# Another execution list for a fused gated-recurrence and GEGLU kernel: which engine runs a step, and in which order all steps are issued

## The chip, the cores and the metric

One Trainium2 chip, one core. The metric is device time of one execution in microseconds, lower is better. The kernel's five queues are TensorE (PE), VectorE (DVE), ScalarE (ACT), GpSimd (POOL) and SyncE (SP); SP and POOL issue the transfers, which 16 DMA engines carry out.

## The reference

Two stages. The first is a recurrence over time with a complex decay, for 4 batches x 8 heads, 768 steps, head size 48:

```python
mag = np.sqrt(a_re * a_re + a_im * a_im)
scale = np.minimum(mag, 0.999) / (mag + 1e-06)
a_re_n, a_im_n = (a_re * scale, a_im * scale)
...
for t in range(S):
    new_re = ar * S_re - ai * S_im
    new_im = ar * S_im + ai * S_re
    S_re, S_im = (new_re + kv, new_im)          # kv = outer(k_t, v_t)
    y[:, :, t] = np.einsum('bhd,bhde->bhe', q[:, :, t], S_re)
```

Its output, as 3072 rows of 384, is x of the second stage (weights 384 x 1536 twice, 1536 x 384, 384 x 384):

```python
gelu = 0.5 * g * (1.0 + erf(g * inv_sqrt2))     # g = x @ w_gate
ffn_out = gelu * (x @ w_val) @ w_out
res_gate = 1.0 / (1.0 + np.exp(-(x @ w_res)))
return (x + res_gate * ffn_out).astype(np.float32)
```

## The kernel before

Time is cut into 6 chunks of 128 rows. A (batch, chunk) pair is a tile of 128 rows by 384 columns, and the 24 tiles are grouped into 14 **units**: units 0 and 1 are chunk 0 of batches 0 and 1, one tile each; unit 2 is chunk 0 of batches 2 and 3; units 3 to 11 have two tiles each, chunk by chunk, batches 0 and 1 and then 2 and 3; units 12 and 13 are the last chunk of batches 2 and 3, one tile each. Every unit goes through three functions, which record steps and don't run them:

- `prepare(p)`: SP loads ar, ai, q, k and v (one transfer of 192 KB for each tile; a letter a or b after the unit names the tile). ACT and DVE make the logarithm of the magnitude and the angle (steps ln, exp, tai, sq, lnb, la, lh, ll, atan, th, tl). PE sums both over the chunk by a triangular matrix (cumL for the logarithm, cumT for the angle; each takes a high and a low part, lh and ll, th and tl). ACT takes exponentials of the sums (pexpE, pexpI), a rounded angle (round, then fr on DVE) and sine and cosine (sin). DVE scales q and k (qe) and spreads them over cosine and sine (feat). For units below 8, PE transposes these features (peT, copied by cpT); from unit 8 on SP does it by transposing transfers (dT). mrd and mrc fetch a chunk's last decay row, carry adds the last angle of the chunk before into the next (both are transfers issued by POOL), vcast converts v.
- `attend(p)`: scores (qk), masking (am), the output of the chunk (av) and its copy (x), the state for the next chunk (kv, U, M, Mc, Gb, Gf).
- `forward(p)`: the transpose of x (peX and cpX for units 0 to 2, SP's dX after that), 12 gv steps of a unit (6 pairs, for w_gate and w_val, L606), gelu (L611) and h (L612), the residual gate (res, tanh), the output product (out, L632), ot (L636), otx (L639) and the store.

`weights()` comes first: POOL issues wg and wv in halves of three pieces of 192 KB each (steps 0 to 11; here wg01 is piece 1 of half 0 of w_gate), wr (step 12) and three pieces of wo (13 to 15). A gv step needs all three pieces of its half.

So there are 1450 steps, numbered as recorded. The order in which they are issued is written out by hand in `ORDER`, and `PLACE` says for steps that could run on several engines which one does. `Plan.run` walks `ORDER`: it gives each tile the buffer of its tag that came free first (25 wide buffers of 128 x 768 for the inputs and intermediates, 8 banks of PSUM), loads ACT's table set where a step needs another one than is loaded ("L" logarithm and exponential, "T" sine and arctangent, "G" gelu and tanh), and issues the step. An engine runs its steps in list order, and a step waits for what it reads and for the readers of the buffer that it takes. Beside that there are turns at a port: steps of the kinds in `PORT` on DVE and POOL wait for the other engine's last such step in the list:

```python
if t.kind in PORT and t.eng in ("DVE", "POOL"):
    other = turn.get("POOL" if t.eng == "DVE" else "DVE")
    if other is not None:
        after(ins, other)
    turn[t.eng] = ins
```

POOL's queue in the first 70 us, by the list (th of unit 5 is th5; tl4 is its low part for unit 4):

```
th0 tl1 mrd1 mrd0 carry3 carry3 wg12 wg11 tl3 carry4 vcast1 tai5 tl4 wg10 wg01 wg02 mrd2 wr mrd3
carry5 wg00 wv00 vcast3 th5 wv10 wv01 tl5 mrc3 wv11 wv12 wv02 wo13 tai6 mrd4 wo14 Gf3 wo15 tai7 ...
```

Of the kernel before, what the change touches and what calls it, by code (L numbers as in the profile page):

```python
# [30 lines left out]
    33: "ACT", 35: "POOL", 50: "DVE", 51: "DVE", 64: "ACT", 114: "DVE", 117: "POOL", 121: "DVE", 129: "ACT", 131: "DVE",  # L31
    134: "ACT", 140: "DVE", 145: "ACT", 190: "DVE", 191: "DVE", 203: "ACT", 213: "DVE", 221: "ACT", 223: "DVE", 227: "DVE",
    228: "DVE", 236: "DVE", 245: "DVE", 305: "DVE", 306: "DVE", 322: "ACT", 323: "POOL", 330: "DVE", 338: "ACT", 340: "DVE",
    422: "DVE", 423: "DVE", 435: "ACT", 438: "ACT", 439: "POOL", 456: "DVE", 460: "DVE", 463: "ACT", 469: "DVE", 479: "DVE",
    554: "POOL", 555: "POOL", 562: "DVE", 572: "DVE", 576: "DVE", 667: "ACT", 670: "POOL", 671: "POOL", 678: "DVE", 686: "ACT",
    692: "DVE", 695: "ACT", 711: "DVE", 783: "ACT", 786: "POOL", 787: "POOL", 794: "DVE", 802: "ACT", 804: "DVE", 821: "DVE",
    872: "DVE", 899: "DVE", 902: "POOL", 903: "POOL", 933: "DVE", 943: "DVE", 978: "DVE", 984: "DVE", 1011: "ACT", 1014: "POOL",
    1033: "DVE", 1035: "ACT", 1050: "DVE", 1088: "DVE", 1124: "POOL", 1125: "POOL", 1132: "DVE", 1143: "ACT", 1198: "DVE",
    1232: "POOL", 1251: "ACT", 1257: "DVE", 1263: "DVE", 1298: "DVE", 1324: "POOL", 1329: "DVE", 1338: "DVE", 1376: "DVE",
    1396: "POOL", 1397: "POOL", 1448: "DVE",  # L40
}
ORDER = [
    97, 98, 16, 17, 102, 103, 294, 180, 179, 104, 105, 21, 178, 293, 22, 106, 23, 107, 24, 25, 295, 296, 108, 26, 109, 110, 34,
    115, 116, 27, 35, 36, 28, 111, 303, 411, 410, 181, 29, 117, 188, 304, 118, 37, 31, 305, 412, 413, 306, 30, 119, 189, 113,
    120, 190, 307, 420, 112, 421, 308, 191, 38, 422, 32, 99, 100, 526, 528, 19, 18, 319, 39, 527, 20, 309, 40, 320, 204, 423,
    114, 122, 321, 125, 310, 8, 436, 41, 42, 205, 7, 314, 182, 529, 300, 121, 124, 123, 44, 206, 192, 126, 207, 43, 46, 322,
    193, 128, 424, 208, 129, 49, 194, 210, 642, 101, 643, 183, 184, 298, 297, 185, 302, 311, 45, 127, 50, 130, 195, 199, 196,
    47, 315, 33, 536, 211, 425, 313, 212, 209, 131, 323, 52, 135, 48, 51, 437, 213, 316, 312, 201, 200, 198, 197, 537, 132, 133,
    324, 137, 56, 136, 57, 538, 141, 54, 138, 214, 134, 53, 55, 139, 327, 325, 216, 58, 438, 299, 645, 301, 326, 140, 142, 439,
    59, 328, 215, 144, 63, 539, 143, 329, 330, 218, 64, 6, 1, 552, 331, 145, 332, 333, 217, 220, 2, 644, 187, 186, 219, 60, 443,  # L50
    440, 334, 540, 335, 652, 441, 226, 222, 341, 336, 221, 202, 12, 317, 553, 0, 3, 345, 653, 62, 442, 223, 342, 227, 61, 759,
    758, 337, 338, 444, 343, 554, 224, 339, 233, 344, 225, 231, 77, 69, 81, 9, 4, 242, 232, 555, 318, 166, 445, 340, 85, 240,
    760, 79, 71, 234, 150, 168, 73, 83, 241, 10, 152, 75, 158, 146, 11, 5, 203, 446, 426, 228, 243, 350, 170, 65, 154, 148, 87,
    67, 13, 156, 364, 761, 171, 559, 235, 427, 541, 160, 89, 560, 162, 654, 90, 431, 351, 236, 164, 348, 428, 561, 349, 244,
    354, 358, 70, 355, 245, 365, 429, 155, 430, 346, 352, 432, 157, 359, 360, 655, 434, 433, 14, 414, 159, 66, 361, 347, 353,
    74, 78, 229, 656, 72, 68, 357, 415, 230, 237, 76, 768, 15, 417, 239, 151, 249, 86, 769, 80, 82, 246, 362, 88, 161, 770, 147,
    153, 250, 149, 238, 84, 251, 556, 668, 91, 163, 252, 771, 669, 416, 167, 557, 363, 657, 165, 448, 784, 447, 558, 367, 261,
    253, 247, 563, 265, 277, 92, 785, 562, 542, 658, 248, 169, 366, 875, 874, 172, 564, 877, 876, 93, 449, 173, 273, 94, 450,
    174, 255, 275, 278, 451, 419, 262, 274, 263, 452, 457, 369, 458, 267, 670, 254, 459, 453, 786, 671, 531, 175, 460, 276, 368,
    884, 435, 455, 266, 476, 474, 885, 264, 454, 987, 418, 530, 532, 477, 475, 456, 772, 886, 268, 257, 269, 279, 270, 466, 271,  # L60
    259, 280, 1097, 986, 1096, 543, 773, 390, 370, 382, 887, 646, 533, 1207, 461, 384, 675, 374, 256, 467, 1099, 386, 774, 392,
    272, 372, 676, 95, 480, 258, 464, 672, 376, 677, 544, 547, 388, 775, 659, 260, 787, 546, 545, 481, 465, 387, 371, 660, 673,
    548, 549, 663, 674, 375, 478, 565, 662, 661, 1206, 96, 468, 287, 1106, 664, 678, 479, 1098, 989, 566, 469, 665, 281, 1107,
    567, 282, 288, 283, 573, 484, 568, 647, 389, 900, 679, 680, 176, 485, 571, 462, 569, 373, 377, 572, 1108, 391, 289, 534,
    394, 988, 284, 570, 648, 290, 996, 681, 383, 463, 649, 666, 901, 1216, 378, 396, 393, 483, 997, 575, 291, 385, 580, 486,
    502, 1217, 535, 574, 576, 998, 498, 581, 380, 504, 397, 582, 590, 177, 1213, 1306, 583, 902, 591, 788, 779, 683, 500, 488,
    789, 592, 470, 506, 487, 356, 395, 999, 791, 593, 490, 792, 285, 577, 471, 790, 379, 776, 689, 508, 492, 903, 489, 381, 793,
    690, 594, 404, 888, 595, 1311, 650, 292, 764, 1208, 651, 765, 550, 682, 685, 584, 405, 881, 684, 781, 586, 406, 601, 889,
    585, 777, 691, 780, 778, 686, 482, 687, 503, 600, 692, 551, 578, 398, 499, 907, 794, 890, 472, 762, 1105, 763, 587, 579,
    1000, 891, 708, 399, 407, 286, 589, 706, 400, 796, 688, 795, 501, 709, 878, 588, 494, 904, 491, 610, 908, 707, 1012, 408,  # L70
    693, 473, 401, 909, 493, 505, 1209, 1378, 510, 628, 606, 1013, 612, 782, 798, 511, 496, 512, 696, 614, 602, 698, 1001, 797,
    513, 629, 883, 905, 618, 697, 402, 604, 667, 622, 906, 620, 699, 1218, 712, 608, 1109, 495, 995, 880, 879, 766, 1307, 409,
    713, 616, 611, 497, 1379, 1214, 767, 596, 624, 892, 895, 710, 694, 507, 619, 613, 1014, 597, 1015, 700, 894, 695, 1383, 896,
    893, 711, 799, 1002, 1312, 897, 913, 701, 800, 914, 716, 715, 509, 1219, 1220, 882, 1212, 514, 603, 1019, 520, 515, 1016,
    605, 621, 599, 1020, 1017, 1110, 1384, 607, 623, 801, 714, 609, 803, 516, 807, 1313, 1385, 625, 1018, 1122, 994, 1021, 804,
    808, 717, 992, 1123, 1221, 802, 910, 403, 1111, 911, 912, 1230, 993, 1102, 702, 521, 805, 522, 615, 742, 636, 703, 523, 598,
    806, 517, 617, 722, 738, 734, 726, 1101, 637, 824, 916, 918, 1103, 920, 1124, 898, 724, 825, 638, 915, 736, 743, 1314, 728,
    812, 718, 822, 740, 813, 809, 626, 639, 627, 735, 1125, 823, 720, 917, 1309, 818, 723, 737, 630, 719, 739, 1126, 814, 727,
    725, 919, 1003, 1222, 1023, 1322, 518, 721, 819, 899, 524, 1004, 741, 826, 1129, 1007, 1315, 729, 519, 525, 705, 921, 1231,
    1127, 1130, 815, 990, 924, 631, 1009, 1131, 1006, 1128, 827, 816, 925, 991, 817, 934, 1005, 1008, 1112, 731, 936, 930, 832,  # L80
    926, 730, 744, 704, 935, 1010, 640, 937, 927, 1026, 745, 1022, 828, 752, 732, 829, 733, 1132, 1380, 833, 1211, 928, 632,
    746, 1323, 783, 810, 1316, 1025, 641, 1024, 753, 938, 747, 811, 922, 748, 858, 1134, 1011, 1133, 1386, 1028, 923, 1030, 939,
    838, 1317, 1027, 1394, 929, 1029, 820, 1113, 633, 749, 945, 1100, 830, 1223, 754, 842, 834, 846, 835, 840, 836, 755, 848,
    844, 1117, 944, 843, 837, 859, 1038, 940, 1224, 1036, 1318, 845, 1114, 831, 854, 1037, 1032, 1031, 1387, 1115, 1232, 941,
    1226, 847, 1039, 1118, 1119, 1225, 756, 849, 958, 1319, 966, 946, 943, 1120, 942, 1320, 1395, 1321, 1116, 1135, 931, 1047,
    950, 954, 1045, 1048, 1215, 1033, 856, 951, 839, 1137, 1381, 1210, 757, 956, 948, 960, 968, 962, 1046, 1233, 634, 952, 841,
# [597 lines left out]
```

## Time and profile before

| | |
|---|---|
| median of 3 runs | 265.2 us (264.7 to 265.84) |
| the profiled execution | 264.54 us, its span 262.7 us |
| granted TensorE clock, mean | 0.974 |
| busy: PE, DVE, ACT, POOL | 226.8, 227.1, 213.8, 91.9 us |
| table loads on ACT | 36, 1.283 us each |
| transfers | 39.83 MB, mean 152 GB/s; SP's queue 75.3% of 16 engines' span, POOL's 9.4% |

The span is from the first to the last instruction of the core. Busy time is the time in which an engine has an instruction under way; matmuls are pipelined, so PE's busy time is more than its work. The page cuts the span into 40 equal slices of 6.57 us and gives each engine's busy share in tenths. "Waits" name, for the idle time ahead of an instruction, what ended it; the chain of waits goes back from the last instruction by whatever released it.

### The profile page before, as it was taken

The page shows a single profiled execution, that of the slowest core. Times are in us where ns is not written, and L with a number is a line of the kernel's source. Part 1 is how long each engine was busy: PE and PEld are TensorE (multiplying, and loading weights), DVE is VectorE, ACT ScalarE, POOL GpSimd, SP SyncE. Part 2 cuts the span into 40 slices and gives each one's busy share as a digit, 9 for nine tenths or more (in the row PEclk, how much of TensorE's full clock was granted, in tenths as well). Part 3 has the DMA queues.
Part 4 walks back from the last instruction along what each step waited for, and adds up shares of the span by engine and source line. Part 5 has one row for each costly group of instructions (what it writes and reads, how often), then busy time and mean ns, then how long its engine had stood idle before and what let it go on. Part 6 is the DMA issues. An engine that isn't in the chain of part 4 may idle for free.

```text
span 262.7 us, 6329 instructions
## 1 busy us (share of the span) xinstructions
PE 226.8 (86%) x2426; PEld 180.7 (69%) x2426; DVE 227.1 (86%) x403; ACT 213.8 (81%) x356; POOL 91.9 (35%) x114
## 2 busy tenths in 40 slices
PE   0332665887999999999999999999999999999993
PEld 0121554775978877887888787778778777887781
DVE  3579899998799999999999999999899997856353
ACT  5999999998999899999999999998798862342330
POOL 1034077495635426652726276042310000200200
PEclk9999995899799999999999999999999999999999
DMA  8999999999998995999999696997989642420202
GB/s 142 187 186 187 200 192 171 197 204 207 196 182 162 171 182 112 217 192 187 168 183 176 122 183 152 135 168 149 180 153 153 127 91 64 107 80 17 91 2 90
DMA packets 162173, 39.83 MB, mean 152 GB/s; under 512 B 155616, under 2 KB 162144, under 8 KB 162144
## 3 DMA queue, kind: packets, MB, share of 16 engines
q1 hardware_dynamic: 157696, 35.53, 75.3%
q0 software_dynamic: 4448, 3.90, 9.4%
q8 instruction: 19, 0.31, 0.5%
q14 instruction: 10, 0.08, 0.1%
HBM read 31.26 MB, written 4.72 MB: 137 GB/s over the span
## 4 chain that ended last, share of the span: by engine, by line
PE 64%; DMA 5%; DVE 4%; ACT 2%; SPq 1%; issue 1%; POOL 0%; DVEq 0%
PE pb L606 32%; PE pb L632 15%; PE pb L621 4%; PE pb L360 3%; PE pb L536 3%; PE pb L505 3%; DMA QT<-fQ 3%; DMA wv<-in_moe_w_val_dram 2%; PE pb L548 1%; PE pb L550 1%; PE pb L560 1%; PE pb L522 1%; DVE fQ L488 1%; DVE Qe L483 1%; ACT h L611 1%
## 5 line engine op out<-in xcount | busy, mean ns | idle before, releaser
L611 ACT ACTIVATE h<-pb 128x512 bf16<-128x512 f32 (+1 forms) x84 | 41.9, 540 | 22.4 <-PE pb L606 22.2
L606 PE MATMUL pb<-xT,wv 128*128 128x256 bf16 (+1 forms) x504 | 58.5, 262 | 1.9 <-DMA wv<-in_moe_w_val_dram 1.9
L612 DVE SCALAR_TENSOR_TENSOR h<-h,pb 128x512 bf16<-128x512 bf16 (+1 forms) x84 | 48.3, 604 | 11.5 <-PE pb L606 8.9
L606 PE MATMUL pb<-xT,wg 128*128 128x256 bf16 (+1 forms) x504 | 56.1, 257 | 0.7 <-DMA wg<-in_moe_w_gate_dram 0.6
L632 PE MATMUL pb<-wo,h 128*128 128x384 bf16 x288 | 55.0, 326 | 0.0
L606 PEld LDWEIGHTS <-wv 128*128 128x128 bf16 x504 | 43.3, 100 | 8.5 <-DMA wv<-in_moe_w_val_dram 2.0
L606 PEld LDWEIGHTS <-wg 128*128 128x128 bf16 x504 | 43.2, 98 | 7.7 <-issue 1.0
L653 ACT ACT_TABLE_LOAD x36 | 46.2, 1283 | 1.3 <-PEq L668 0.7
L632 PEld LDWEIGHTS <-h 128*128 128x128 bf16 x288 | 26.0, 97 | 13.3 <-issue 0.5
L539 DVE TENSOR_TENSOR am<-pb,mask 128x512 bf16<-128x512 f32 x48 | 32.1, 682 | 1.6 <-PE pb L536 1.6
L639 POOL TENSOR_TENSOR ot<-ot,x 128x384 f32<-128x384 f32 x16 | 14.6, 914 | 45.2 <-DVE ot L636 20.9
L360 PE MATMUL pb<-lh,ut_one 128*128 128x384 f32 x24 | 10.6, 442 | 15.9 <-DVE lh L407 15.9
L536 PE MATMUL pb<-QT,KT 96*128 96x128 bf16 x192 | 18.1, 219 | 1.6 <-DMA QT<-fQ 0.8
L453 POOL TENSOR_TENSOR tl<-t,th 128x768 fp32r<-128x768 f32 (+1 forms) x9 | 14.8, 1641 | 13.2 <-DVE la L404 8.4
L335 POOL CAST v<-vf 128x768 bf16<-128x768 f32 (+1 forms) x8 | 6.0, 746 | 33.1 <-DVE ot L639 28.7
L636 DVE SCALAR_TENSOR_TENSOR ot<-sg,pb 128x384 f32<-128x384 f32 x24 | 13.0, 547 | 4.9 <-PE pb L632 3.7
L360 PEld LDWEIGHTS pb<-lh,ut_one 128*128 128x128 f32 x24 | 5.0, 207 | 17.4 <-DVE lh L407 16.8
L536 PEld LDWEIGHTS <-KT 96*128 96x128 bf16 x192 | 12.6, 97 | 5.1 <-issue 2.8
L573 POOL TENSOR_TENSOR Gf<-U,M 96x384 f32<-96x384 f32 x9 | 7.4, 824 | 23.8 <-DVE ll L409 13.6
L335 POOL CAST th<-t 128x768 fp32r<-128x768 f32 (+1 forms) x10 | 7.2, 725 | 24.0 <-DVE fK L488 11.6
L623 ACT ACTIVATE sg<-pb 128x384 f32<-128x384 f32 x24 | 11.7, 500 | 4.7 <-DVE ot L636 3.1
L398 POOL TENSOR_TENSOR t<-t,ai 128x768 f32<-128x768 f32 (+1 forms) x9 | 14.7, 1632 | 2.1 <-PE pb L606 1.1
(91 smaller groups left out, 492.0 us busy)
## 6 DMA issues: line engine op xcount, KB each, us to landing
ar<-in_a_re_dram SPq DMA_DIRECT2D x24, 192.0 KB, 4.6
ai<-in_a_im_dram SPq DMA_DIRECT2D x24, 192.0 KB, 4.6
q<-in_q_dram SPq DMA_DIRECT2D x24, 192.0 KB, 4.6
k<-in_k_dram SPq DMA_DIRECT2D x24, 192.0 KB, 4.3
vf<-in_v_dram SPq DMA_DIRECT2D x24, 192.0 KB, 4.2
out_dram<-ot SPq DMA_DIRECT2D x24, 192.0 KB, 2.6
wg<-in_moe_w_gate_dram POOLq DMA_DIRECT2D x6, 192.0 KB, 5.7
wv<-in_moe_w_val_dram POOLq DMA_DIRECT2D x6, 192.0 KB, 5.6
```

What stands on the lines that cost most here:

```text
L335: return on[eng].tensor_copy(out=out, in_=in_)
L360: nc.tensor.matmul(out=bank.tile, lhsT=ut_one, rhs=x[:, i * DM:(i + 1) * DM], start=(j == 0), stop=(j == 1))
L398: add(e1, "tai", lambda: on[e1].tensor_tensor(out=F("t"), in0=F("t"), in1=flat(T("ai"), n), op=OP.mult), [s["ai"]], [s["t"]], n)
L453: add(e10, "tl", lambda: on[e10].tensor_tensor(out=F("tl"), in0=F("t"), in1=F("th").bitcast(FP), op=OP.subtract), [s["t"], s["th"]], [s["t ...
L536: nc.tensor.matmul(out=ap.tile[:, h, :], lhsT=kT.tile[0:DD, u * H // 2 + h, :], rhs=qT.tile[0:DD, u * H // 2 + h, :], start=True, stop=True)
L539: add("DVE", "am", lambda u=u, am=am, ap=ap: nc.vector.tensor_tensor(out=am.tile[:, u * H // 2:(u + 1) * H // 2, :], in0=ap.tile, in1=mask ...
L606: nc.tensor.matmul(out=o_.tile[:, u, :], lhsT=w_[:, k_, (2 * m + u) * 128:(2 * m + u + 1) * 128], rhs=s["xT"].tile[:, k_, 0:n].rearrange(" ...
L611: add("ACT", "gelu", lambda gp=gp, hv=hv: nc.scalar.activation(out=hv(), in_=gp.tile, func=AF.Gelu), [gp], [hh], n, "G")
L612: add("DVE", "h", lambda vp=vp, hv=hv: nc.vector.scalar_tensor_tensor(out=hv(), in0=hv(), scalar=0.5, in1=vp.tile, op0=OP.mult, op1=OP.mul ...
L632: nc.tensor.matmul(out=op_.tile, lhsT=s["h2"].tile[:, k_, i * 128:(i + 1) * 128], rhs=wo[:, k_, :], start=(k_ == 0), stop=(k_ == NF - 1))
L639: add(e8, "otx", lambda i=i, ot=ot, e8=e8: on[e8].tensor_tensor(out=ot.tile, in0=ot.tile, in1=s["x"].tile[:, i].rearrange("p h d -> p (h d ...
L653: plan.run(ORDER, lambda table: nc.scalar.preload_act_table_set(ACT_SETS[table]), after)
```

## The change

Both tables are replaced; nothing else in the file changes. The steps, their arithmetic, the buffers (`WD = 25`, 8 banks), the units, the split between PE and transfers for transposes, and the rule of the turns stay. 75 steps run on another engine: copies of x 6 from DVE to ACT and 6 back, cpT 5 and 5, abs 4 and 4; three tl and three vcast go from DVE to POOL, two tl from POOL to DVE; the rest are single th, mrc, Mc, sq, tai, otx and Gf steps. The order differs from the third step on.

```diff
 PLACE = {
-    33: "ACT", 35: "POOL", 50: "DVE", 51: "DVE", 64: "ACT", 114: "DVE", 117: "POOL", 121: "DVE", 129: "ACT", 131: "DVE",
...
+    24: "DVE", 33: "DVE", 40: "DVE", 50: "DVE", 51: "ACT", 53: "ACT", 64: "ACT", 104: "POOL", 114: "ACT", 116: "POOL",
...
 ORDER = [
-    97, 98, 16, 17, 102, 103, 294, 180, 179, 104, 105, 21, 178, 293, 22, 106, 23, 107, 24, 25, 295, 296, 108, 26, 109, 110, 34,
-    115, 116, 27, 35, 36, 28, 111, 303, 411, 410, 181, 29, 117, 188, 304, 118, 37, 31, 305, 412, 413, 306, 30, 119, 189, 113,
...
+    97, 98, 16, 102, 293, 17, 103, 410, 104, 21, 105, 22, 106, 294, 23, 24, 411, 179, 115, 295, 34, 35, 116, 296, 117, 107, 25,
+    178, 118, 303, 26, 36, 420, 27, 37, 108, 119, 28, 100, 181, 180, 413, 304, 109, 120, 421, 110, 305, 121, 38, 29, 188, 30,
...
```

By name, POOL's queue becomes:

```
tai1 th1 mrd0 carry3 carry3 mrd1 tl3 wg01 carry4 tai5 wg11 th4 mrd2 wg02 wr wg12 carry5 wg10 wg00
th5 tl5 vcast2 mrd3 wv02 wv01 tai6 wv00 wv10 wv11 wv12 wo13 tai7 wo14 Gf3 wo15 Gf3 mrd4 ...
```

and SP's first 46 transfers, before and after (named input, unit, tile):

```
before: ar1 ai1 ar0 ai0 ar3b ai2a ar2b ar2a ar3a ai3a ai3b ar4b ar4a ai2b ai4a ai4b q1 k1 ar5a ai5a k0 q0 ar5b vf0
        q2a ai5b k3b ar6a vf1 ar6b q2b k2a q3b q3a k2b vf3b k3a ai6b vf3a ai6a vf2b vf2a ar7b ar7a ai7a ai7b
after:  ar1 ai1 ar0 ar3a ai0 ar4a ar3b ar4b ar2b ai3a ai3b ar2a k1 ai2b ai2a ai4b ai4a q1 q2a vf1 ar5a k0 q0 q2b
        k3a ar5b ai5a vf0 ai5b k2a k2b q3b k3b ar7b q3a vf2a ar7a ar6b ar6a vf2b ai7b ai6b ai6a vf3a vf3b ai7a
```

## The prediction

> **What bounds the kernel now.** I read the busy row, the slices, a table by stage, the chain of waits around 58 us, and POOL in order of time. Each engine runs its steps in list order, so the n-th instruction of an engine in the trace is the n-th step of that engine in the list, and every step has a measured start.
>
> ```profile
> PE 226.8 (86%) x2426; PEld 180.7 (69%) x2426; DVE 227.1 (86%) x403; ACT 213.8 (81%) x356; POOL 91.9 (35%) x114
> PE   0332665887999999999999999999999999999993
> PEclk9999995899799999999999999999999999999999
> ```
>
> PE has its holes in the first eleven slices (72 us) and none after. The table by stage (length, busy time and count of PE, PEld, DVE, ACT, POOL, then granted clock, DMA share, GB/s) says the same, and that DVE and ACT are full from 30 us on:
>
> ```profile
> 10.00:30.00 20.00, 7.57 (x26) 4.47 (x27) 15.58 (x26) 19.70 (x30) 5.76 (x8) 1.00 1.40 190
> 30.00:50.00 20.00, 14.30 (x134) 11.35 (x132) 19.77 (x34) 19.10 (x34) 12.94 (x15) 0.74 1.08 186
> 50.00:70.00 20.00, 16.91 (x255) 14.99 (x255) 16.89 (x33) 18.54 (x35) 12.99 (x16) 0.91 1.22 204
> 70.00:100.00 30.00, 30.00 (x327) 24.18 (x325) 30.00 (x54) 28.10 (x45) 12.15 (x11) 1.00 0.96 166
> 100.00:160.00 60.00, 59.75 (x661) 48.58 (x659) 59.45 (x99) 59.49 (x97) 32.68 (x36) 1.00 0.94 179
> ```
>
> To make this a sum I take PE's own work from start to start: the tenth percentile, by kind, of the time from one step's first matmul to the next step's. 120 gv steps of two chunks at 0.652 us, 48 of one at 0.335, 72 out at 0.647, 24 res at 0.487, 48 qk at 0.220, 28 peT at 0.446, 24 cumL at 0.350, 24 cumT at 0.435, 20 av at 0.406, 20 kv at 0.203, and 4.4 for the rest: 211.0 us. I call **lag** the start of a PE step less the PE work listed ahead of it. In before it is 8.35 at the first matmul, 38.1 at 51.6 us (first qk of unit 2), 39.6 at 61.6, 41.7 at 64.0, 43.4 at 71.4 (first out), 44.2 at 100.4, 44.8 at 157.4, 46.6 at 193.8 and 47.4 at the last matmul's end, 258.45. Then 4.25 us follow (ot, otx, store). 211.0 + 47.4 + 4.25 = 262.7, the span; the execution's 264.54 is 1.84 more, and the median 265.2 another 0.66. So the lag is all that a list can change: 43.4 of it is made before 71 us, 4.0 after.
>
> The step from 39.6 to 43.4 is one wait. The chain of waits:
>
> ```profile
> 56.72 1.23 POOL wv L341 x2
> 57.95 5.98 DMA wv<-in_moe_w_val_dram
> 63.92 0.05 issue
> 63.97 0.73 PE pb L606 x10
> ```
>
> The first step that reads wv stands until its third piece has landed. It left so late because POOL's queue was held up (start, length, and in brackets the idle time before and what ended it):
>
> ```profile
> 46.26 0.88 POOL L440 DMA_DIRECT2D t<-fr  x1
> 52.91 0.83 POOL L335 CAST th<-t 128x768 fp32r<-128x768 f32 x1 [2.46 <-DMA t<-fr]
> 53.68 1.07 POOL L341 DMA_DIRECT2D wv<-in_moe_w_val_dram  x2
> 54.74 1.84 POOL L453 TENSOR_TENSOR tl<-t,th 128x768 fp32r<-128x768 f32 x1
> 56.66 1.83 POOL L341 DMA_DIRECT2D wv<-in_moe_w_val_dram  x3
> ```
>
> The carry that th waits for was issued at 46.3 behind six transfers and landed at 52.6. PE's wait is 2.05 us; then the clock falls (granted 0.50 in 66 to 68 us) and four gv steps take 0.64 instead of 0.335: 1.2 more.
>
> **The change, by queue.** No instruction goes or comes, table loads are 36 in both lists; 75 steps change engine. With slots from start to start (DVE 128x768 from SBUF 0.87, am, h and cpT 0.60; ACT 0.73 to 0.83; a table load 1.18; POOL 1.76), DVE's sum goes from 219.3 to 217.5, ACT's from 198.2 to 199.3, POOL's from 82.9 to 85.6. None is a gain by itself; what counts is how much of each queue stands ahead of a PE step, more than PE work does.
>
> *Start.* In before, DVE has stood idle for 12.1 us when tl of unit 2 ends at 27.6, ACT for 5.2 at 29.9. In the new list I follow the queues by the landing times of before (the n-th load of SP lands at 3.6 + 1.04(n-1) us up to the 24th). tai of unit 1 on POOL costs 1.0 instead of 0.55, th and tl come ahead of la: the last ll of units 0 and 1 ends at 14.3 (13.2 before). But ai of unit 2 is 15th instead of 14th and ACT's exp of unit 2 follows without a hole, so tai of unit 2 runs 19.6 to 20.5, ACT finishes atan of unit 4 at 25.9 with 21.5 us of slots behind it (4.4 idle), and DVE's tl of unit 2 ends at 26.4 with 15.1 (11.3 idle). The later waits that I could follow (tl of unit 3 on POOL 31.1 to 32.9, under two cpT and two fr of DVE; tai5 34.3 to 36.1; th4 from 38.0) end before DVE or ACT needs them; idle time is then some 11.9 on DVE and 5.5 on ACT at 50 us (before: 12.7 and 6.8).
>
> *What stands ahead of PE.* DVE's slots ahead of a PE step exceed PE's by at most 27.2 (qk of unit 3, PE work 17.7): lag at least 39.2. ACT's by 32.8 (gv at 17.9): at least 38.4. Before: 26.6 and 31.8 in the same stretch. So without the weights PE stands at a lag of 39.2 to 39.8 here, as before (39.6). There is no gain in this part.
>
> *Weights.* New POOL order: carry5, two wg, th5, tl5, vcast2, mrd3, wv02, wv01, tai6, wv00, wv10, wv11, wv12, wo. Four transfers (mr of unit 2, wg02, wr, wg12) now leave near 40 us, ahead of carry5, where there were six. carry5 leaves when atan5 is done (37.5 + 5.3: 42.8) and lands near 47.5; th5 also has the port to wait for, until feat3 on DVE ends at 48.9. th5, tl5 (0.8 + 1.8) to 51.6; vcast2 waits for its v load, 40th on SP: 3.6 + 39 x 1.04 + 7.5 weight pieces x 1.04 = 52.0; it ends at 52.9; wv02 and wv01 leave by 54.3. tai6 waits for ai6a, 43rd: 55.2, and ends at 57.1, so wv00 leaves at 57.5, about when the last wv piece left before. Issue to landing of the six wv was 7.6, 4.7, 5.8, 5.1, 5.4 and 6.0; with one piece just ahead I take 5.3: 62.8 (from 62.2 to 65.1, and to 66.9 if ai6a is 2 us late too). It is first needed at PE work 21.8: lag 41.0. wv12 lands near 66 and is needed at 24.8 (65.8 at this lag); the wo pieces near 68, 71 and 73.5 are needed at 69, 72 and 75. So PE waits 1.5 us instead of 2.05 and does so earlier in its work. For the clock I add 0.3 of the 1.2 seen: **lag 41.3 against 43.4**.
>
> A rule of the Trainium skill bears on that 0.3: "TensorE: Matmul & The Clock Gate", What's actually happening, has the clock fall only after an idle window of about 3.4 us. The trace does not agree, since 1.87 us of idle PE before 63.97 was followed by a granted 0.50; by the page the term would be 0 and the lag 41.0.
>
> *Middle and end.* From here all three engines are nearly full, and a PE step slips where another queue has more work between two points than PE has. In before the worst such stretch on DVE, from Mc of unit 2 (68.5) to qk of unit 5, holds 0.57 us more than PE's; the worst on ACT 0.36 more. In the new list DVE's tightest stretch has 0.35 to spare, ACT's worst lacks 0.30. Overall DVE's excess over PE in the middle falls from 27.6 to 26.1: with 13 to 14 us of idle time that is a lag of 40.1, under 41.3, so DVE no longer paces PE. Around 173 to 179 us PE lost 1.2 on transposed Q and K of unit 9 that landed 0.2 and 0.1 us before their use; DVE's excess ahead of that step falls from 22.5 to 19.2. So of the 4.0 after 71 us, 0.6 and 1.2 go; for places that these sums don't see I put back 1.0 (nothing, or up to 4 as in all of before): 3.2. The tail is the same two instructions and a store, 4.25.
>
> Sum: lag 44.5, span 211.0 + 44.5 + 4.25 = 259.75, execution 261.6, and with the 0.66 to the median **262.2**.
>
> **Rivals.**
> *More is won.* If wv00 is there by 61.1, PE never waits (lag 39.4) and only 2.2 comes later: 41.6, 259.3. For it: one wv landed in 4.7. Against: even so ai6a has to land 1.1 us earlier than its place on SP says.
> *The gain is given back.* If DVE stands idle as long as before (16.4 us at 69), its 26.7 of excess at PE work 32 gives 43.1, and with 4.0 later 47.1: 264.9. For it: three engines at full, a shared port, 1.1 us more ACT work, tl and vcast moved to POOL where DVE waits for them. Against: 2.6 of the 16.4 came behind the wv wait itself.
> *Slower: the weights behind tai6.* wv00 now stands behind a multiply that waits for a load, and loads stall while POOL's transfers run (before, SP's load 40 landed at 49.8 and 41 at 54.3). With ai6a at 57 and 7.6 to land, 66.9: lag 45.1, the full clock loss 1.2, and 3.2: 49.5, or 267.2. It turns slower from a landing of about 66.2 on.
>
> **Chances.** Forecast 0.50 (own range 260.3 to 263.9), more won 0.12, given back 0.22, slower 0.16. About 0.5% (1.3 us) is what a measurement can tell from no change, so: faster 0.62, same 0.22, slower 0.16. Range: from 259.3, the low rival, to 267.2, the top of the wv bound.
>
> **What will show it.** Right: the first wv matmul of PE starts near 62.8 with 1 to 2 us idle before it, ended by a wv transfer; wv00 leaves POOL near 57.5; DVE idle near 12 us at 50; the first out matmul near 69.5; PE without holes from 70 to the end; the last matmul near 255.5. Wrong: a granted clock of 0.5 for longer after 62 us, PE holes after 75 us behind a tai, otx or tl of POOL or a late load, or a first wv matmul after 66.

## The result, and the profile after

The new list takes **261.88 us** (median of 4 runs, 261.35 to 262.78) against 265.22 for the kernel before, measured beside it: a ratio of 0.9877, 95% interval 0.984 to 0.9913. On a second chip it took 262.05 against 263.97: 0.9931, from 0.9895 to 0.9968. The profiled execution took 262.78 us, the highest of its four, with a span of 261.0; the second chip's profiled one took 261.91 with a span of 260.0. The forecast was 262.2, with 261.6 and 259.75 for one profiled execution and its span. Against a forecast gain of 3.0 us the medians differ by 3.3 on the first chip and by 1.9 on the second, on which the kernel before was itself 1.25 us faster.

The page's busy row and two of its slice rows:

```profile
PE 226.4 (87%) x2426; PEld 181.8 (70%) x2426; DVE 225.4 (86%) x404; ACT 214.1 (82%) x355; POOL 94.5 (36%) x114
PE   0230992889999999999999999999999999999993
PEclk9999996599999999999999999999999999999998
```

The holes of PE now lie in the first nine slices (before: the first ten; the prediction counted eleven), and the clock has no second dip behind them (before: 7 in the eleventh slice). The table by stage:

```profile
30.00:50.00 20.00, 13.80 (x118) 11.40 (x116) 18.67 (x30) 19.05 (x32) 10.80 (x13) 0.78 1.27 197
50.00:70.00 20.00, 18.66 (x279) 15.91 (x278) 18.98 (x38) 18.25 (x37) 13.90 (x15) 0.96 1.10 193
70.00:100.00 30.00, 29.95 (x330) 24.52 (x328) 29.34 (x52) 29.49 (x50) 13.15 (x14) 1.00 1.15 179
100.00:160.00 60.00, 60.00 (x667) 49.13 (x665) 59.66 (x103) 58.91 (x93) 34.85 (x37) 1.00 0.90 168
```

From 30 to 50 us PE got *less* done than before (118 matmuls against 134) and DVE stood 1.3 us instead of 0.2; from 50 to 70 us it got more (279 against 255). So the gain is made in one stage, against a loss in the stage before it. The clock column can't be compared there: a view counts the time ahead of the first entry of the trace's clock record as 1.00, and that entry, a rise to 1.00, lies at 37.79 us here and at 31.40 in the profile of before. What PE's rate was until then is seen below, at c0. The chain of waits shows the weights:

```profile
49.77 5.38 DMA ai<-in_a_im_dram
...
55.64 1.10 POOL wv L340 x2
56.73 1.76 POOL t L397
58.50 5.66 DMA wv<-in_moe_w_val_dram
```

ai of unit 6, then tai6 on POOL, then wv00: the order that the prediction followed. Times of single steps in the prediction's walk, and in what answers it here, count from 0.24 us after the span's start, the lines of the profile from the start; in the walk's count wv00 left at 58.3 and landed at 63.9, 0.8 and 1.1 us later than forecast. In before, the last piece that PE waits for landed at 63.7 in the same count: in this execution the weights came no earlier. PE came later, waited 0.6 us there instead of 2.05, and no slower clock followed.

For all runs I use the **lag** of the prediction, the start of a PE step less the PE work listed ahead of it. The columns are points of PE work in us; 14.2 is a time of some 54 us, 21.7 lies just ahead of the first step that reads wv in before and at it in after, 28 is the first out, 209 the last steps (the last matmul's end, counted from the span's start as in the prediction, adds 0.4, of which 0.24 is that count). The first profile is of the run above.

| run | span | 14.2 | 21.7 | 22.5 | 28 | 120 | 209 | growth from 28 |
|---|---|---|---|---|---|---|---|---|
| before | 262.7 | 39.3 | 39.6 | 41.8 | 43.4 | 45.0 | 47.0 | 3.6 |
| after, first profile | 261.0 | 41.1 | 42.2 | 42.3 | 42.6 | 43.8 | 45.3 | 2.7 |
| c0 after, second chip | 260.0 | 39.9 | 40.6 | 40.6 | 41.6 | 42.8 | 44.3 | 2.7 |
| e1 before, wv early | 260.5 | 39.7 | 40.5 | 40.8 | 41.3 | 43.0 | 44.7 | 3.4 |
| e2 after, wv late | 264.5 | 40.0 | 44.4 | 45.5 | 46.2 | 47.2 | 48.8 | 2.6 |
| e3 after, wv early | 261.1 | 39.6 | 40.1 | 40.2 | 41.0 | 42.0 | 45.3 | 4.3 |
| e13 the same again | 261.1 | 41.4 | 41.9 | 42.0 | 42.7 | 43.7 | 45.4 | 2.7 |
| e6 after, extra transposes | 261.5 | 40.4 | 41.6 | 41.7 | 42.0 | 43.3 | 45.8 | 3.8 |
| e7 and wv early | 261.6 | 40.8 | 42.1 | 42.2 | 42.8 | 43.8 | 45.9 | 3.1 |
| e4 new order alone | 274.9 | 47.7 | 48.8 | 48.9 | 49.2 | 55.8 | 59.5 | 10.3 |
| e5 new engines alone | 270.6 | 41.4 | 42.1 | 42.5 | 43.4 | 50.0 | 54.8 | 11.4 |
| e10 head of after | 263.4 | 40.7 | 41.9 | 42.0 | 42.4 | 45.6 | 48.0 | 5.6 |
| e11 head of before | 264.3 | 38.5 | 39.0 | 41.2 | 42.8 | 46.2 | 48.9 | 6.1 |
| e12 e1's head | 267.0 | 40.3 | 40.5 | 40.8 | 41.2 | 46.6 | 51.6 | 10.4 |

Each row is one execution, and before was profiled on the first chip alone. Two executions of one list (after and c0, e3 and e13) differ by 1.2 and 1.8 at 14.2 and by 1.0 and 0.1 at 209; differences between rows of that size show nothing by themselves.

### The profile page after: what moved, and what is told of

Same layout as the page of the kernel before. It is cut to its first block, busy times and chain, and to the rows that moved or that the text cites. A ratio compares the mean times of both kernels' runs of the same rounds, so it can differ in the third digit from the quotient of the medians.

```text
span 261.0 us, 6358 instructions
## 1 busy us (share of the span) xinstructions
PE 226.4 (87%) x2426; PEld 181.8 (70%) x2426; DVE 225.4 (86%) x404; ACT 214.1 (82%) x355; POOL 94.5 (36%) x114
## 4 chain that ended last, share of the span: by engine, by line
PE 71%; DMA 11%; ACT 9%; DVE 3%; POOL 2%; SPq 1%; issue 1%; POOLq 0%; DVEq 0%
PE pb L605 32%; PE pb L631 17%; PE pb L359 6%; PE pb L620 4%; PE pb L504 4%; PE pb L535 3%; DMA wo<-in_moe_w_out_dram 3%; DMA wv<-in_moe_w_val_dram 2%; DMA ai<-in_a_im_dram 2%; ACT L652 2%; DMA t<-fr 2%; DMA ar<-in_a_re_dram 2%; POOL t L397 1%; PE pb L549 1%; PE pb L547 1%; ACT CS L477 1%
## 5 line engine op out<-in xcount | busy, mean ns | idle before, releaser
L610 ACT ACTIVATE h<-pb 128x512 bf16<-128x512 f32 (+1 forms) x84 | 41.2, 547 | 23.2 <-PE pb L631 13.0
L631 PE MATMUL pb<-wo,h 128*128 128x384 bf16 x288 | 56.5, 326 | 0.0
L652 ACT ACT_TABLE_LOAD x36 | 46.2, 1283 | 1.3 <-PEq L667 0.7
L605 PEld LDWEIGHTS <-wv 128*128 128x128 bf16 x504 | 41.9, 98 | 7.5 <-issue 1.3
L631 PEld LDWEIGHTS <-h 128*128 128x128 bf16 x288 | 26.3, 97 | 13.0 <-issue 0.4
L397 POOL TENSOR_TENSOR t<-t,ai 128x768 f32<-128x768 f32 (+1 forms) x10 | 16.0, 1601 | 18.1 <-DVE fK L487 9.0
L504 PE MATMUL pb<-ident,fK 128*128 128x128 bf16 x112 | 10.0, 246 | 13.5 <-DVE fK L487 13.5
L359 PE MATMUL pb<-th,ut_one 128*128 128x384 f32 x24 | 11.3, 471 | 11.4 <-POOL th L334 11.1
L452 POOL TENSOR_TENSOR tl<-t,th 128x768 fp32r<-128x768 f32 (+1 forms) x10 | 16.5, 1656 | 10.4 <-DVE ll L408 7.8
L504 PEld LDWEIGHTS <-fK 128*128 128x128 bf16 x112 | 8.4, 112 | 15.0 <-DVE fK L487 14.3
L535 PEld LDWEIGHTS <-KT 96*128 96x128 bf16 x192 | 13.8, 101 | 3.9 <-issue 2.2
L620 PE MATMUL pb<-wr,xT 128*128 128x384 bf16 x72 | 15.5, 326 | 0.0
L423 ACT ACTIVATE E<-pb 128x384 f32<-128x384 f32 x24 | 11.5, 500 | 3.2 <-PE pb L359 3.0
```

Source lines behind the costliest of these rows:

```text
L359: nc.tensor.matmul(out=bank.tile, lhsT=ut_one, rhs=x[:, i * DM:(i + 1) * DM], start=(j == 0), stop=(j == 1))
L397: add(e1, "tai", lambda: on[e1].tensor_tensor(out=F("t"), in0=F("t"), in1=flat(T("ai"), n), op=OP.mult), [s["ai"]], [s["t"]], n)
L452: add(e10, "tl", lambda: on[e10].tensor_tensor(out=F("tl"), in0=F("t"), in1=F("th").bitcast(FP), op=OP.subtract), [s["t"], s["th"]], [s["t ...
L504: nc.tensor.transpose(out=tp.tile[:, h, :], in_=s[g].tile[:, i * H + h], identity=ident)
L535: nc.tensor.matmul(out=ap.tile[:, h, :], lhsT=kT.tile[0:DD, u * H // 2 + h, :], rhs=qT.tile[0:DD, u * H // 2 + h, :], start=True, stop=True)
L605: nc.tensor.matmul(out=o_.tile[:, u, :], lhsT=w_[:, k_, (2 * m + u) * 128:(2 * m + u + 1) * 128], rhs=s["xT"].tile[:, k_, 0:n].rearrange(" ...
```

## Experiments

The theory after the result: the gain comes from the value weights, whose landing PE reaches with little or no wait and so with no slower clock behind it; a smaller part comes from less growth later. The rivals: the gain is in the new list as a whole, or is given by the engines or the order alone.

### c0: the changed kernel once more

> The changed kernel once more, for a second profile beside the kernel before. Both theories: a median of 261.4 to 262.8 us. If the profiled execution is again at the upper end (lag of PE at its first wv step 42.2, at the end 45.4), the first profile is typical; if it lies near 261.4, I expect the difference in the first 60 us, where PE, DVE and ACT wait for transfers, not after 75 us.

Measured: 262.05 us, 0.9931 (0.9895 to 0.9968), growth 2.7 as in the first profile, but a lag of 39.9 instead of 41.1 at 14.2. The list is the same, so the 1.2 us are no property of it. The groups by line from 31 to 38 us (mean ns of one matmul after the comma) show where they are, first in the first profile:

```profile
L359 PE MATMUL pb<-lh,ut_one 128*128 128x384 f32 x3 | 1.9, 626 | 0.0
L535 PE MATMUL pb<-QT,KT 96*128 96x128 bf16 x12 | 1.5, 315 | 0.0
```

and in c0:

```profile
L535 PE MATMUL pb<-QT,KT 96*128 96x128 bf16 x16 | 1.4, 220 | 0.7 <-DVE KT L334 0.7
L359 PE MATMUL pb<-lh,ut_one 128*128 128x384 f32 x3 | 1.2, 399 | 0.0
```

The same matmuls take 626 against 399 ns and 315 against 220. In c0 PE steps come at their full rate from some 32.5 us on, in the first profile from some 38. The clock is what differs: the trace's clock record has its first entry, the rise to 1.00, at 32.10 us in c0 and at 37.79 in the first profile, though a view gives 1.00 for the whole stretch in both. DVE pays too, in the first profile's order of time:

```profile
37.28 1.29 DVE L538 TENSOR_TENSOR am<-pb,mask 128x512 bf16<-128x512 f32 x2 [1.19 <-PE pb L535]
```

This mask waits 1.19 us for scores of the slow PE; in c0 it starts at 35.72 and waits for nothing.

### e1 to e3: the place of the weights alone

e1 is before with steps 4 and 5 (wv01, wv02) directly behind 3 (wv00); e2 and e3 are after with step 3 later or earlier.

```diff
 e1, before:  ... 553, 0, 3,
+e1:          4, 5,
 e2, after:   ... 874, 4, 654,
-e2:          3,
 e2:          ... 9, 10, 168, 446, 11,
+e2:          3,
 e3, after:   ... 874, 4,
+e3:          3,
 e3:          654,
-e3:          3,
```

> The list of before, with two weight transfers (wv01, wv02) issued straight behind wv00 and ahead of vcast3, th5 and tl5. Lag theory: the 2.05 us wait of PE at its first wv step goes, and with it the 1.2 us of half clock; the lag at the first out step falls from 43.4 to about 40.8 (DVE's excess 26.9 and 13.8 idle), and as PE then stays full, most of it reaches the end: 262.6 us (262 to 263.5). Rival, given back: DVE paces the middle, its idle time grows elsewhere, the lag at the end is again 47: 264.6 or more. Second rival: the loads that these two push back (two pieces, 2.1 us, for v of unit 2) cost as much as they bring: 265 or more.

> The changed list, with wv00 issued last of the wv pieces, behind wv12. It should land near 67.3 instead of 63.9, and PE's first wv step needs it at PE work 21.8. Lag theory: PE waits 3.4 us longer, and as PE is what ends everything, all of it reaches the end: 265.3 us, or 266.5 if the clock falls to half behind a wait this long (1.2 us more). Rival: the queues behind have slack, or DVE paces the middle: under 263.5.

> The changed list, with wv00 issued ahead of tai6, straight behind wv01. Lag theory: only the 0.6 us that PE still waited there can go, since its lag was already 41.6 from the idle time of DVE and a slow clock of PE before it: 261.3 us, at best 0.6 under the changed kernel. Rival, that the weights are what sets the lag as I predicted (a wait of 1.5 us): 1.0 to 1.5 under it, 260.4 to 260.9.

Measured on one chip: e1 262.58 us, 0.9931 (0.99 to 0.9962); e2 266.76, 1.0099 (1.0064 to 1.0134); e3 261.67, 0.9899 (0.9854 to 0.9944). e1 and e2 came as the lag theory had them (262.6, and 266.5 with a slower clock). The tables by stage, 62 to 70 us, of before, after, e1, and (66 to 68) e2:

```profile
62.00:70.00 8.00, 6.13 (x87) 5.67 (x86) 5.41 (x14) 6.84 (x12) 4.55 (x6) 0.79 1.26 201
```

```profile
62.00:70.00 8.00, 7.57 (x127) 6.69 (x124) 6.98 (x16) 7.28 (x17) 3.65 (x4) 1.00 1.22 203
```

```profile
62.00:70.00 8.00, 7.88 (x149) 7.06 (x148) 8.00 (x23) 7.93 (x12) 5.73 (x6) 1.00 1.14 175
```

```profile
66.00:68.00 2.00, 1.55 (x10) 1.25 (x11) 0.00 (x0) 0.00 (x0) 0.00 (x0) 0.55 1.26 188
```

Two steps moved in before's list raise the matmuls of that stretch from 87 to 149, keep the clock at 1.00 and take the lag at the first out from 43.4 to 41.3. In time they gain as much as the whole change does on that chip: 0.9931 for both. In e2 the same piece, landing at 66.2, stops PE, DVE and ACT (PE's waits name it):

```profile
PE pb L606 <- DMA wv<-in_moe_w_val_dram: 3.8, 1, 3.8
```

and the lag ends 4.5 above c0, in a list that is otherwise that of after. So the weights' place carries the result in both directions. e3 is the case that doesn't fit in size: a lag 0.5 under c0's where wv is first read, and still 0.6 under it at the first out, but 45.3 at the end. Its waits of PE from 172 to 196 us:

```profile
PE pb L536 <- DMA KT<-fK: 1.2, 1, 1.2
PE pb L536 <- DMA QT<-fQ: 0.9, 1, 0.9
```

and the issue of the later Q on SP:

```profile
170.56 1.31 SPq L497 DMA_TRANSPOSE QT<-fQ  x1
```

This transposing transfer of Q of unit 9 had its input at 161.4 and was issued behind other entries of SP's queue at 170.6, only 1.3 us earlier than in the first profile of after, while PE came about 1.8 us earlier. A PE that is early there waits for SP. The other wait, 1.2 us for K of unit 10, has another cause: that transfer took 5.4 us from issue to landing, against 3.3 in the first profile and in c0. So more than half of these two waits is a spread of one transfer, whose cause stays open.

### e4 and e5: order or engines alone

e4 has the new `ORDER` with the old `PLACE`, e5 the old `ORDER` with the new `PLACE`.

> The new order with the old table of engines. If the order makes the gain (fewer waits at the start and at the weights, better stretches in the middle), the time lies within 1 us of the changed kernel's 261.9. Rival, order and engines only work together: DVE then has 1.8 us more work and copies stand on engines that the order left no room for: 264 or more, slower than before if DVE's excess over PE goes back over 27.5 with the idle time of the changed kernel (13.9): 263.5 to 267.

> The old order with the new table of engines. DVE has 1.8 us less, but its order was made for the other split. If the engines make the gain: 263 or less. If the two tables only work together: 266 to 270, with PE holes after 75 us where a copy now stands behind a long ACT or POOL step.

Measured: e4 277.58 us, 1.0506 (1.0456 to 1.0555); e5 272.8, 1.0335 (1.0286 to 1.0383). The lag of e4 is 8.4 over before already at 14.2 and grows by 10.3 from the first out; e5 is 2.1 over before at 14.2 and level with it at the first out, where before has had its wait for wv, and grows by 11.4 behind it. So neither table brings a part of the gain by itself: a step put on another engine needs the order that was made for it, and 75 of 1450 steps are enough to cost 3 to 5%.

### e6 and e7: transposes ahead of the first peT, to have PE at full rate

110 transposes of the identity are added ahead of the first feature transpose, into the bank that this one then overwrites; e7 has wv00 early as well.

```diff
+WARM = {(1, 0, "K"): 110}
...
                     tp.make([128, H, 128], BF)
+                    for _ in range(WARM.get((p, i, g), 0)):
+                        nc.tensor.transpose(out=tp.tile[:, 0, :], in_=ident, identity=ident)
                     for h in range(H):
```

> The changed kernel with 110 extra transposes of the identity on PE ahead of the first peT of unit 1, in time in which PE stands idle (16 to 25 us); what they write is overwritten by the peT itself. In the changed kernel PE's steps from 25.8 to 38 us took twice their usual time (a peT 0.82 instead of 0.45 from start to start), though the record of the granted clock shows 1.00 there, and DVE then waited 1.2 us for a score step. If that is a clock that has not risen yet: peT at 0.45 from the first on, DVE's wait gone, lag before the first wv step down from 41.6 to about 40.4; then PE waits there for wv00, which lands at 63.9 as before: little or no gain at the end, 261.4 to 261.9. If these steps were slow for another reason (operands, ports), nothing changes before 38 us.

> Both edits: the extra transposes ahead of the first peT, and wv00 ahead of tai6. Lag theory: with either alone the other wait takes its place; with both the lag at the first out step falls from 42.6 to about 41 and the end by as much: 260.2 us (259.8 to 261). Rival, given back: no better than the better of the two alone, 261.3.

Measured: 263.47 us, 0.996 (0.9935 to 0.9986), and 263.09, 0.994 (0.9915 to 0.9966): the expected gain did not come (the changed list without the transposes: 0.9877 and 0.9931). The transposes themselves show the rise of the clock. In e7 they start 107 ns apart up to 19.86 us, the first entry of the clock record, and 56 ns apart behind it (in e6 the same, at 17.84); the counts of PE, in equal stretches, with 1.00 as the clock in both:

```profile
15.70:19.80 4.10, 4.10 (x40) 4.10 (x40) 2.80 (x5) 4.10 (x8) 0.70 (x1) 1.00 1.40 185
19.90:23.90 4.00, 4.00 (x73) 3.90 (x70) 4.00 (x7) 3.97 (x7) 1.50 (x3) 1.00 1.41 191
```

PE of e7 behind them in order of time, then its clock (the column ahead of the last two in the table by stage):

```profile
25.96 0.62 PE L508 MATMUL pb<-ident,fK 128*128 128x128 bf16 x8 [1.99 <-DVE fK L489]
26.39 0.42 PE L361 MATMUL pb<-th,ut_one 128*128 128x384 f32 x1
28.48 0.69 PE L361 MATMUL pb<-tl,ut_one 128*128 128x384 f32 x1 [1.66 <-DVE tl L454]
```

```profile
26.00:28.00 2.00, 0.81 (x9) 0.56 (x9) 0.54 (x1) 1.98 (x3) 0.00 (x0) 0.67 0.82 155
28.00:30.00 2.00, 1.44 (x5) 0.94 (x6) 2.00 (x5) 0.85 (x2) 0.00 (x0) 0.50 1.04 193
```

The first eight transposes do run at full rate (0.62 us; 1.04 in c0), but PE stands 1.99 us ahead of them, for DVE's feature K, and 1.66 behind them, for DVE's tl, and the clock falls. The work that would have used the rate is not there yet. Later in e7, between 30 and 66 us, PE still waits 0.7 for a cast of v on POOL and 0.6 for wv.

### e10 to e12: head and rest of the lists

The first 510 steps (to PE work 47 or 48, some 90 us) of one list, then all other steps in the order of the other, each step on the engine that its list gives it. The two heads differ by 10 steps. e12 has e1's head.

```diff
 e10:  ORDER = after[:510]  + [j for j in before if j not in after[:510]]
 e11:  ORDER = before[:510] + [j for j in after  if j not in before[:510]]
 e12:  ORDER = e1[:510]     + [j for j in after  if j not in e1[:510]]
```

> The first 510 steps of the new list (to PE work 48 us, some 91 us of time) with the new engines, then all other steps in the order and on the engines of before. Theory (two separate gains): the head gives its lag, 41.9 to 42.9 at PE work 50, and the rest grows as in before, 3.3 from there: lag 45.2 to 46.2 at the end, 1.0 to 1.8 us under before. Rival A (all of the gain is made in the rest, the head is only a spread of the executions): as before, 0 to -0.3. Rival B (a list only works as a whole, and the seam, at which 10 steps stand on the other side, costs as much as a mixture of list and engines did): 5 us or more over before.

> The other half: the first 510 steps of before's list, then the new list. Theory: lag 43.5 to 43.7 at PE work 50 with the wait for the value weights and the slower clock behind it, then a growth of 2.4 as in the new list: 46.0 at the end, 0.9 us under before. Rival A (all in the rest): as the new list, 1.8 to 3.3 under before. Rival B (the seam): 5 us or more over before.

> The same with wv01 and wv02 moved directly behind wv00 in the head of before, so that the wait is gone: lag 41.3 to 41.5 at PE work 50, and a growth of 2.4: 43.7 to 43.9 at the end, 3.1 us under before, 0.4 to 1.4 under the new list as it is. If the growth belongs to what the head leaves behind in the queues and not to the rest of the list, it stays at 3.2 as in before: 44.7, as with that head and before's rest.

Measured: 265.77 us, 1.0044 (1.0005 to 1.0082); 266.63, 1.0101 (1.0064 to 1.0138); 268.09, 1.0124 (1.006 to 1.0187). All three are slower than before. PE's waits of e10, e11 and e12 behind the seam:

```profile
PE pb L506 <- DVE fQ L489: 1.7, 1, 1.7
```

```profile
PE pb L548 <- DVE am L539: 1.6, 1, 1.6
PE pb L606 <- DMA xT<-x: 1.1, 1, 1.1
```

```profile
PE pb L606 <- DVE h L612: 2.1, 1, 2.1
```

In e12 the first wait of e11 is there too, and behind its own of 2.1 the granted clock was 0.57 from 180 to 184 us. e10 keeps its head's gain (lag 42.6 at PE work 50, against 43.7 in before), loses 2.5 within the next 10 us of work at the seam, and then grows by 2.9 to the end, like before (2.6). e11 and e12 fail the theory: the rest of the new list grows by 4.1 and 8.3 from 50 on behind the other head, not by 2.4. So these mixtures do not show the smaller growth as a gain that the rest of the list carries with it. Whether they lose it to the other head or to the seam, behind which each of them waits, they can't tell apart, and which steps the 0.9 less growth belongs to stays open.

### e13: e3 for a second profile

> The new list with wv00 ahead of tai6 once more, for a second profile. In its first profile the lag was 41.0 at PE work 28 and 41.2 at 60, but rose by 3.9 between 120 and 180, twice as much as in the list itself. If that late loss belongs to the list (PE arriving earlier meets transposes that are not earlier), it shows again at the same steps, growth 4.2, and the time is within 0.5 us of the new list. If it was a spread of that execution, the growth is 2.4 to 2.7 and the time 1.2 to 1.6 us under the new list.

Measured: 262.15 us, 0.9894 (0.9829 to 0.9959). This execution had the slow start (lh matmuls 626 ns, lag 41.4 at 14.2) and grew by 2.7, with a single late wait of 0.6. Together with e3: an early execution lost 4.3 later, a late one 2.7, and both end at 45.3 and 45.4, as the first profile of after does. So an early PE gives part back to late transfers on SP, but c0, early and at 44.3, shows that this floor is not firm. Neither e3 nor e13 can be told from the list as it is (0.9877 and 0.9931).

## Why the prediction was right, and where it was wrong

The time was right to 0.3 us, and part of that is luck. The forecast span of 259.75 missed the profiled 261.0 by 1.25; the steps from a profiled execution to the median, put at +0.66 as in before, came to -0.90, since the profiled execution was the highest of its four. By the prediction's own steps, for the first profile and for c0:

| step | forecast | first profile | c0 |
|---|---|---|---|
| lag ahead of the wv wait | 39.5 | 41.6 | 40.4 |
| PE waits for wv (start to start) | 1.5 | 0.6 | 0.1 |
| from there to the first out (clock term 0.3) | 0.3 | 0.4 | 1.1 |
| growth to the end of the last matmul | 3.2 | 3.1 | 3.1 |
| tail | 4.25 | 4.3 | 4.3 |
| sum with PE's 211.0 | 259.75 | 261.0 | 260.0 |

*PE's work as the measure, and the lag as all that a list can change:* held; the sum closes for both profiles.

*Start:* the walk by landing times was good while it followed transfers and DVE (last ll ended at 14.3, tai of unit 2 at 20.7, atan of unit 4 at 26.3; forecast 14.3, 20.5, 25.9). It missed one wait, that of tl of unit 2 for the carry that overwrites t:

```profile
26.87 0.96 DVE L452 TENSOR_TENSOR tl<-t,th 128x768 fp32r<-128x768 f32 x1 [0.83 <-DMA t<-fr]
```

The carry landed at 26.5, so tl ended at 27.6, not 26.4, and DVE's idle time there was 12.4 instead of 11.3.

*What stands ahead of PE, "a lag of 39.2 to 39.8":* this step failed (the table has it at 39.5), by 2.1 us in the first profile and 0.9 in c0, for two reasons. The first is PE's own rate. The bound took DVE's idle time as 11.9 at 50 us; it was 13.9 at 37.7 us in the first profile. The step durations were tenth percentiles of the whole run, and from 26 us to the rise of the clock at 32 or 38 us PE works at some half to two thirds of that rate (peT 0.82 us from step to step, not 0.446). The share of the rate is shown by c0 and e13, where the same list, or the same up to 56 us, gives a lag of 39.9 or 41.4 with the lh matmuls at 399 or 626 ns. The second reason is in both profiles: the output steps (av) of unit 2 wait, in the first profile for vcast2, in c0 for a copy of K by ACT.

```profile
55.22 0.36 PE L547 MATMUL pb<-v,am 128*128 128x48 bf16 x8 [0.61 <-POOL v L334]
54.06 0.36 PE L547 MATMUL pb<-v,am 128*128 128x48 bf16 x8 [0.62 <-ACT KT L333]
```

Ahead of this step the lag is 40.3 in the first profile and 39.1 in c0, where the bound held until then. The step and the second av of the unit, which waits 0.2 for its mask, add 1.1 in both. The bound by DVE's and ACT's queues had no term for them.

*Weights:* the order of events was right, with one link for another: carry5 left at 44.2 (42.8 by the walk), feat3 ended at 51.4 (48.9) and so th5 and tl5 came late, vcast2 ended at 54.9 (52.9) behind tl5 and not behind its v load (landed at 52.6), ai6a landed at 54.9 (55.2), tai6 ended at 58.3 (57.1), wv00 landed at 63.9 (62.8); in c0 57.3 and 62.3. The wait was mis-sized for a reason that the sum contained: the landing is a floor, so every us that PE is late ahead of it is one less to wait there. So the two errors are largely one: +2.1 and -0.9 in the first profile, +0.9 and -1.4 in c0. What is left of them, +1.2 and -0.5, is the error of the landing, 1.1 late and 0.5 early.

In c0 a further 0.8 over the forecast went between the first wv step and the first out, and these are later floors of the same kind. A gv step lost 0.4 within itself until wv12 had landed, at 65.9 (66 by the walk), and the first out waited for the first piece of wo, issued at 60.2 and landed at 69.7 (68 by the walk).

*Clock term 0.3:* no fall was seen behind waits of 0 to 0.4 us as the profile counts them; before's 1.9 and e2's 3.8 were followed by one.

*Growth 3.2:* right in size, 3.1. The stretch that was to gain 0.6 (PE work 28 to 60) went from 1.0 to 0.4; at the transposes of unit 9, where 1.2 was to go, it went from 1.7 to 1.0 (120 to 140), since one wait of 0.4 to 0.5 for Q stayed. The 1.0 put back for unseen places covered that.

*Rivals:* "the weights behind tai6" did not come, but e2 built it: by the prediction's sum a landing at 66.2 gives 44.4 + 1.2 + 3.2 = 48.8, or 266.5 us; e2 took 266.76 in the median and 266.42 in the profiled execution. "More is won" asked for a PE that never waits for wv; c0 had that and e3 nearly (0.4), and still they came to 260.0 and 261.1 in the span (256.9 by that rival), because the lag was not 39.4 and the growth not 2.2. "Given back" did not come.

## What to carry to other kernels

Read the wait that stands last ahead of the full stage, and first try the few steps that it hangs on: two steps moved in the old list gave, on the chip where both ran, as much as a new list of 1450. A landing is a floor, so don't add a delay and the wait behind it as two terms; and check the start for the rate at which PE really ran, not the rate of the whole run. An order and its engines are one plan: half of a better plan was 3 to 5% slower than the old one.

## What the runs showed of the hardware

One list, two starts: matmuls of 128x384 in f32 took 626 ns in two (after, e13) and 399 to 406 ns in four (c0, e2, e3, e10) of six executions of this start, from 31 to 38 us. The clock records of the traces hold the cause: their first entry, the rise to 1.00, lies at 37.79 and 38.16 us in the two and at 31.99 to 32.22 in the four. Ahead of its first entry the record is empty and a view gives 1.00, so the sign to go by is the time of one matmul form, 107 and 56 ns from start to start on the two sides of the rise in e6 and e7. "TensorE: Matmul & The Clock Gate" of the Trainium skill, section What's actually happening, has the array start throttled and be released after a free-running window of about 3.4 us of work, so that the number of slow matmuls varies from run to run, at under 1% of a span. The trace agrees in kind (between two executions of one list the lag at 14.2 differs by up to 1.8 us, 0.7% of 261; the record's stretches between two entries last 3.41 us or a whole multiple of it). It does not agree with a fall only after an idle window of that length: in e7 the record falls to 0.50 at 26.69 us, behind a wait of 1.99 us and eight transposes, and in before at 65.53, behind a wait of 1.87.
